# The second feed-forward's weights are split in token chunks 1 to 4, parked in DRAM, and fetched in chunk 5

## The chip, the core and the metric

The kernel runs on one core of a Trainium2 chip. The metric is the device time in microseconds (us) of one execution; each kernel is timed in several runs, and the median is quoted. A profile is one execution of its own, and its span runs from the first instruction to the last.

The engines are named as the profile names them: PE is TensorE (matmuls), DVE is VectorE, ACT is ScalarE, POOL is GpSimd, and SP is SyncE, which issues the DMAs here. Every engine works through its own instructions in the order in which they are written; an instruction that waits for a semaphore holds up all that stand behind it on that engine.

## What is computed

Three blocks follow one another, on 2304 tokens (4 batches of 576) of width 512 (8 heads of 64):

```python
q_s = softmax(q, axis=-1);  k_s = softmax(k, axis=2)         # a linear attention
x   = einsum(q_s, einsum(k_s, v))                            # [2304, 512]
xn  = x / rms(x) * rms_g                                     # first feed-forward, 1536 wide
x   = (silu(xn @ w_gate) * (xn @ w_val)) @ w_out
h   = x @ w_in                                               # second feed-forward, 2048 wide
P   = a[0] + a[1]*h + a[2]*h**2 + a[3]*h**3
Q   = 1.0 + abs(b[0])*abs(h) + abs(b[1])*h**2
out = (P / (Q + 1e-6)) @ w_out2
```

The feed-forward weights come as float64 arrays, q, k and v as float32.

## The kernel before

**Precision.** A product of two float32 matrices is made of three matmuls: each operand is split into a high and a low half that TensorE multiplies exactly (type fp32r), and high x high, high x low and low x high add up in PSUM (`mm3`, `proj`, `emit_y`, `o_pe`). So every operand exists as two tiles: x as X[c][0] and X[c][1], the product of gate and value as uh and ul, the rational function's result as gh and gl.

**Weights.** A weight tile is 128 x 512. The first feed-forward has 36 of them (W1: gate g, value v and output o of 12 steps f), the second 32 (W2: i for w_in and o for w_out, of 16 steps). A tile is loaded as float64 words (512 KB), put into a slot of 4 KB per partition (`tag=f"s{i % N1}"`, 36 slots) and converted there: two operations on the words (`conv_exp` on ACT, `conv_low` on ACT or DVE), the sign and the joining of the words on DVE (`conv_sign`, `conv_join`), the high half on ACT or DVE (`conv_hi`) and the low half on POOL (`conv_lo`). The split form takes over the slot. Since W1 fills all 36 slots, W2's tiles come into slots whose W1 tile was read for the last time, which is in the last chunk.

**Chunks and steps.** The tokens go in 6 chunks of 384. Chunk 0 is written out by hand as a list of events (ORDER), with the conversion of all of W1 in it. Chunks 1 to 5 run a loop over 12 steps f (`u_step`): the group g of 12 matmuls, silu on ACT, the group vv of 12 matmuls, the product u on DVE, its halves uh (ACT) and ul (DVE; POOL in chunk 5), and then the projection y of the step before, 12 matmuls (`emit_y`). Into three positions of every step the attention of the next chunk is woven (`schedule`): maxima, exponentials and sums on DVE and ACT, the small matmuls kv, xq and xx on PE. Chunks 2 and 3 compute the k and v part for a new batch in two halves of four heads; kv of the first half stands in step 4, of the second half in step 5. All v of the batch's second half goes into the one tile `vt0`, so its load (`load_v`) stands behind the first half's kv. A chunk's y goes to DRAM (`y_d`).

In chunk 5 there is no next attention. At the start of every step `load_to` issues the loads of W2 whose slots are free, and `tick` (`conv_tick`) puts one conversion further in three places of the step. What is left of the conversion runs in the second feed-forward (`conv_steps`, one operation of DVE a step).

**Second feed-forward.** A loop over 96 steps s (6 chunks of 16): h (12 matmuls, `h_pe`), the rational function on ACT and DVE (`rational`, six operations on each), gh on ACT and gl on POOL (`c_split`), and three steps later the output o (9 matmuls, `o_pe`).

Nothing but the written order decides what runs next: there is no scheduler. In what follows, tile i of W2 in a chunk's staging is called tile n.

Of the kernel before, what the change touches and what calls it, by code (L numbers as in the profile page):

```python
# [9 lines left out]
F32 = mybir.dt.float32  # L10
# [37 lines left out]
def kernel(  # L48
# [30 lines left out]
    # ln's argument is kept inside the table's range for every float32 denominator  # L79
# [20 lines left out]

    def ps(name):
        return pw.tile([P, 512], F32, tag="pw", name=name)

# [7 lines left out]
    # a 4 KB slot for each tile, which its split form takes over from its float64 form  # L111
# [8 lines left out]
    done = dict.fromkeys(("load", "a", "b", "c"), 0)  # L120
# [18 lines left out]

    def words(i):  # L140
        raw = raws[i]
        return (
            raw.bitcast(U32).rearrange("p (m t) -> p m t", t=2),
            raw.bitcast(F32).rearrange("p (m t) -> p m t", t=2),
        )

    # float64 words (low, high) to float32, rounded
    def conv_exp(i):
        w, r = words(i)
        # the exponent's bias goes from 1023 to 127; what float32 can't hold goes to zero  # L150
        nc.scalar.activation(r[:, :, 1], r[:, :, 1], AF.Copy, scale=2.0 ** -112)
# [42 lines left out]
    def conv_tick(end):  # L194
        """One tile further in each of three stages."""
        a, b, c = (done[k] for k in "abc")
        go_b = b < a
        if c < b:
            conv_hi(c)
            conv_lo(c)  # L200
            done["c"] += 1
        if go_b:
            conv_sign(b)
        if a < min(end, done["load"]):
            conv_exp(a)
            conv_low(a)
            done["a"] += 1
        if go_b:
            conv_join(b)
            done["b"] += 1  # L210

    def conv_steps():
        """What is left of the conversion, one operation of the vector engine at a time."""
        a, b, c = (done[k] for k in "abc")
        for i in range(c, len(order)):
            if i >= a:
                conv_exp(i)
                conv_low(i)
                yield
            if i >= b:  # L220
                conv_sign(i)
                conv_join(i)
                yield
            conv_hi(i)
            conv_lo(i)

# [5 lines left out]
    # five 6 KB slots: this chunk's two halves, the next one's q, x, and halves  # L232
# [18 lines left out]
    def runs(c):  # L251
        """Pieces of a chunk by batch: (batch, offset in the chunk, first row, rows)."""
        t0, end = c * T, (c + 1) * T
        while t0 < end:
            b, s = divmod(t0, S)
            n = min(end - t0, S - s)
            yield b, t0 - c * T, s, n
            t0 += n
# [4 lines left out]
    # four heads at a time, as two pairs: row s of head h of a pair is on partition  # L263
    # D * h + s // SC
# [18 lines left out]
    # token TT * p + t of the chunk is on partition p, in column t * P + p when turned  # L283
# [176 lines left out]
    # 1 / rms by token: Newton's steps from the exponent's half  # L460
# [33 lines left out]
    # the same for every partition at once, where the vector engine has the time  # L494
# [53 lines left out]
    def with_bank(evs, name):  # L548
        """Tensor-engine parts into one bank, then the rest."""
# [21 lines left out]
    def schedule(c):  # L571
        """By position (three in a step of the first feed-forward): what to emit there."""
# [90 lines left out]
    def u_step(c, f, at_pos, tick, lo_eng):  # L663
# [7 lines left out]
        tick()  # L671
# [4 lines left out]
        tick()  # L676
# [3 lines left out]
        tick()  # L680

# [49 lines left out]
    def ab_dve(s0, s1):  # L731
        """The last three of step s0 and the first three of step s1, in turn."""
# [55 lines left out]
    with tc.manual_schedule():  # L788
        # the first chunk's attention, with the first weights behind it
# [9 lines left out]
        # the tensor engine's clock rises only under load  # L799
# [5 lines left out]
        # The first chunk, in ORDER: events of the attention of chunk 0 (a..), of chunk 1 (b..),  # L805
        # of the weights (l: load up to a tile, c..: conversion), and of the feed-forward's steps
# [54 lines left out]
        # attention, of batch 0 for chunk 0 and of batch 1 for chunk 1  # L861
# [23 lines left out]
        # chunk 0: x before its scaling by token serves the first two steps  # L885
# [62 lines left out]
        # chunk 1's x  # L948
# [12 lines left out]
        # chunk 0's steps  # L961
# [37 lines left out]
        done.update(a=N1, b=N1, c=N1)  # L999

        for c in range(1, NCH):
# [5 lines left out]
            else:  # L1007
# [7 lines left out]
                # the second one's first steps run under the end of the first  # L1015
# [3 lines left out]
            for f in range(F1):  # L1019
                tick = lambda: None  # L1020
                if last:
                    # into slots of tiles that an earlier step was the last to read
                    load_to(N1 + min(max(0, 3 * f - 1), 2 * F2))
                    tick = (lambda: conv_tick(len(order))) if f < F1 - 1 else (lambda: None)
# [3 lines left out]
        rest = conv_steps()  # L1028
        n_h = 3
        for s in range(2, len(steps) + 3):  # L1030
# [11 lines left out]
            if s > 2:  # L1042
                next(rest, None)
# [35 lines left out]
```

## Time and profile before

| | us |
|---|---|
| median of 3 runs | 1022.33 (1022.26 to 1022.91) |
| the profiled execution, span | 1019.5 |
| PE busy | 962.4 (94%) |
| DVE busy | 713.7 (70%) |
| ACT busy | 561.6 (55%) |
| POOL busy | 284.5 (28%) |
| chunk 0 | 0 to 167.4 |
| chunks 1, 2, 3, 4 start | 167.4, 246.9, 335.7, 424.5 |
| chunk 5 starts | 504.0 |

The profiled execution's own time is not listed apart from its span; the median of the runs is 2.8 us longer than the span. Matmuls are pipelined and their ends are modelled, so a busy PE may still not be one at its peak: the distance from the start of one matmul to the start of the next tells more than the busy time. The granted clock is TensorE's, 1.00 for 2.4 GHz and 0.5 for 1.2 GHz. An idle time of an engine in the rows stands in brackets with what ended it.

### The profile page before, as it was taken

How to read it: one execution, taken by the hardware profiler on the slowest of the kernel's cores; microseconds unless marked ns; L12 is line 12 of the kernel's file. 1: busy time of each engine (PE TensorE's matmuls, PEld its weight loads, DVE VectorE, ACT ScalarE, POOL GpSimd, SP SyncE). 2: the span in 40 equal slices, each digit the busy share in tenths (PEclk: the TensorE clock that was granted, in tenths of full speed). 3: DMA queues.
4: the chain of work that ended last, by engine and by line, in shares of the span. 5: the costliest groups of instructions: out<-in, count | busy, mean ns of one | idle time of the engine just before them, and what ended most of it. 6: DMA issues, size and time to landing. Idle time of an engine off the chain costs nothing.

```text
span 1019.5 us, 14130 instructions
## 1 busy us (share of the span) xinstructions
PE 962.4 (94%) x5408; PEld 896.2 (88%) x5408; DVE 713.7 (70%) x1160; ACT 561.6 (55%) x1037; POOL 284.5 (28%) x240
## 2 busy tenths in 40 slices
PE   7877779999999999999998889899999999999998
PEld 7775778999999999999997877699999999999997
DVE  5799996436535643633569989987777777777776
ACT  2565553322312232232244557788888888878876
POOL 2565534000000000000047753432423324224222
PEclk7799989999999999999999889999999999999999
DMA  8993002003010410100085521001010010100000
GB/s 213 352 312 114 1 1 69 18 1 78 32 48 1 109 25 1 47 16 1 32 280 183 166 63 63 1 1 63 1 63 1 1 63 1 40 23 1 32 1 31
DMA packets 57491, 64.87 MB, mean 64 GB/s; under 512 B 21328, under 2 KB 47952, under 8 KB 57424
## 3 DMA queue, kind: packets, MB, share of 16 engines
q1 hardware_dynamic: 57424, 63.98, 20.6%
q8 instruction: 42, 0.69, 0.3%
q14 instruction: 25, 0.20, 0.1%
HBM read 54.53 MB, written 9.44 MB: 63 GB/s over the span
## 4 chain that ended last, share of the span: by engine, by line
PE 70%; DVE 20%; issue 6%; ACT 2%; DMA 1%; POOL 0%; DVEq 0%; SPq 0%; ACTq 0%
DVE raw L165 6%; PE o L768 6%; PE o L767 6%; PE o L766 6%; PE h L615 6%; PE h L613 6%; PE h L614 6%; DVE tmp L172 4%; PE g L613 3%; PE vv L613 3%; PE vv L615 3%; PE g L615 3%; PE g L614 3%; PE vv L614 3%; PE y L614 3%
## 5 line engine op out<-in xcount | busy, mean ns | idle before, releaser
L754 POOL TENSOR_TENSOR gl<-t,gh 128x384 fp32r<-128x384 f32 x94 | 105.7, 1124 | 245.5 <-ACT gh L752 207.1
L615 PE MATMUL h<-y,w 128*128 128x384 f32 x384 | 129.5, 337 | 0.0
L613 PE MATMUL h<-y,w 128*128 128x384 f32 x384 | 129.3, 337 | 0.0
L614 PE MATMUL h<-y,w 128*128 128x384 f32 x384 | 128.9, 336 | 0.0
L190 POOL TENSOR_TENSOR w<-tmp,w 128x512 fp32r<-128x512 f32 x68 | 104.8, 1546 | 82.7 <-ACT w L184 41.4
L727 DVE SCALAR_TENSOR_TENSOR A<-S,absb,A 128x384 f32<-128x384 f32 x96 | 62.7, 653 | 80.8 <-ACT A L717 80.8
L768 PE MATMUL o<-w,gl 128*128 128x512 f32 x288 | 114.8, 399 | 3.3 <-POOL gl L754 3.2
L651 ACT ACTIVATE uh<-u 128x384 fp32r<-128x384 f32 x72 | 37.8, 525 | 145.4 <-DVE u L660 126.3
L766 PE MATMUL o<-w,gh 128*128 128x512 f32 x288 | 112.5, 391 | 2.3 <-ACT gh L752 2.3
L767 PE MATMUL o<-w,gh 128*128 128x512 f32 x288 | 113.7, 395 | 0.0
L614 PE MATMUL y<-ul,w 128*128 128x384 f32 x288 | 100.7, 350 | 11.7 <-POOL ul L656 7.3
L613 PE MATMUL y<-uh,w 128*128 128x384 f32 x288 | 101.7, 353 | 9.9 <-ACT uh L651 9.8
L660 DVE TENSOR_TENSOR u<-u,vv 128x384 f32<-128x384 f32 x60 | 33.1, 551 | 108.1 <-PE vv L615 95.8
L656 POOL TENSOR_TENSOR ul<-u,uh 128x384 fp32r<-128x384 f32 x18 | 21.2, 1180 | 306.0 <-ACT uh L651 305.8
L613 PE MATMUL g<-x,w 128*128 128x384 f32 x280 | 98.9, 353 | 3.3 <-DVE w L182 3.1
L615 PE MATMUL g<-x,w 128*128 128x384 f32 x280 | 96.2, 344 | 3.4 <-POOL w L190 3.4
L615 PE MATMUL y<-uh,w 128*128 128x384 f32 x288 | 99.3, 345 | 0.0
L614 PE MATMUL g<-x,w 128*128 128x384 f32 x280 | 96.2, 343 | 0.0
L667 ACT ACTIVATE u<-g 128x384 f32<-128x384 f32 x60 | 29.3, 488 | 102.0 <-PE g L615 102.0
L613 PE MATMUL vv<-x,w 128*128 128x384 f32 x240 | 81.1, 338 | 0.0
L615 PE MATMUL vv<-x,w 128*128 128x384 f32 x240 | 80.3, 335 | 0.0
L614 PE MATMUL vv<-x,w 128*128 128x384 f32 x240 | 80.2, 334 | 0.0
(190 smaller groups left out, 2389.1 us busy)
## 6 DMA issues: line engine op xcount, KB each, us to landing
raw<-in_moe_w_out_dram SPq DMA_DIRECT2D x28, 512.0 KB, 6.0
raw<-in_moe_w_in_dram SPq DMA_DIRECT2D x16, 512.0 KB, 4.2
raw<-in_moe_w_gate_dram SPq DMA_DIRECT2D x12, 512.0 KB, 9.3
raw<-in_moe_w_val_dram SPq DMA_DIRECT2D x12, 512.0 KB, 10.5
k<-in_k_dram SPq DMA_DIRECT2D x8, 576.0 KB, 5.7
v<-in_v_dram SPq DMA_DIRECT2D x16, 288.0 KB, 6.7
y_d<-y SPq DMA_DIRECT2D x6, 768.0 KB, 3.5
yr<-y_d SPq DMA_DIRECT2D x6, 768.0 KB, 4.5
```

The costliest lines, as they stand in the source:

```text
L165: nc.vector.tensor_scalar(out=h[:, :, 1], in0=h[:, :, 3], scalar1=0x8000, scalar2=None, op0=ALU.bitwise_and)
L172: nc.vector.scalar_tensor_tensor(out=tmps[i], in0=w[:, :, 1], scalar=3, in1=w[:, :, 0], op0=ALU.logical_shift_left, op1=ALU.bitwise_or,)
L190: nc.gpsimd.tensor_tensor(out=t[:, 1, :], in0=tmps.pop(i).bitcast(F32), in1=t[:, 0, :], op=ALU.subtract)
L613: nc.tensor.matmul(o, lhsT=lh, rhs=rh, start=start, stop=False)
L614: nc.tensor.matmul(o, lhsT=lh, rhs=rl, start=False, stop=False)
L615: nc.tensor.matmul(o, lhsT=ll, rhs=rh, start=False, stop=stop)
L651: nc.scalar.activation(uh, u, AF.Copy)
L727: nc.vector.scalar_tensor_tensor(out=out, in0=in0, scalar=scalar, in1=in1, op0=op0, op1=op1)
L754: eng.tensor_tensor(out=r["gl"], in0=r["t"], in1=r["gh"], op=ALU.subtract)
L766: nc.tensor.matmul(o, lhsT=r["gh"][:, ts], rhs=w[:, 0], start=first, stop=False)
L767: nc.tensor.matmul(o, lhsT=r["gh"][:, ts], rhs=w[:, 1], start=False, stop=False)
L768: nc.tensor.matmul(o, lhsT=r["gl"][:, ts], rhs=w[:, 0], start=False, stop=last)
```

## The change

W2 is no longer converted in chunk 5 and behind it. Chunk 0 ends with four stores (`park`) of the split W1 tiles in slots 0 to 3 (gate and value of steps 0 and 1) to DRAM. In each of chunks 1 to 4, once steps 0 and 1 have read these slots, eight tiles of W2 pass through them, one a step: load into slot 0 or 1 (`stage_load`), both operations on the words on ACT (`stage_words`), sign and join on DVE (`stage_join`), high half on ACT and low half on DVE into slot 2 or 3, and a store to DRAM (`stage_split`, `park`). A tile takes three steps. In steps 8 to 11 the four W1 tiles are fetched back for the next chunk. In chunk 5, `fetch_to` reads the split tiles from DRAM into the slots where `load_to` put the float64 words; `conv_tick` and `conv_steps` are gone. The number of matmuls is the same, and so are ORDER and the second feed-forward.

```diff
+    split_d = {}
...
-    done = dict.fromkeys(("load", "a", "b", "c"), 0)
+    done = {"load": 0}
...
+    def park(i, t):
+        split_d[i] = dram.tile([P, 2, 512], F32, name=f"sd_{i}")
+        nc.sync.dma_start(out=split_d[i], in_=t.bitcast(F32))
+
+    def fetch(i):
+        dct, which, f = order[i]
+        t = wp.tile([P, 2, 512], F32R, tag=f"s{i % N1}", name=f"wf_{i}")
+        nc.sync.dma_start(out=t.bitcast(F32), in_=split_d[i])
+        dct[which, f] = t
+
+    def fetch_to(n):
+        while done["load"] < n:
+            fetch(done["load"])
+            done["load"] += 1
...
-    def conv_tick(end):
...
-    def conv_steps():
...
+    PARK = 2 * F2 // (NCH - 2)
+
+    def stage_load(c, n):
+        i = N1 + PARK * (c - 1) + n
+        dct, which, f = order[i]
+        src = w_rows(w_out2, f) if which == "o" else w_cols(w_in2, f)
+        raw = wp.tile([P, 512], U64, tag=f"s{n % 2}", name=f"raw_{i}")
+        dst = raw.rearrange("p (c m) -> p c m", m=P) if len(src.shape) == 3 else raw
+        nc.sync.dma_start(out=dst, in_=src)
+        raws[i] = raw
+
+    def stage_words(c, n):
+        i = N1 + PARK * (c - 1) + n
+        conv_exp(i)
+        w, r = words(i)
+        nc.scalar.activation(w[:, :, 0], w[:, :, 0], AF.Copy, scale=7.49 * 2.0 ** -32)
+
+    def stage_join(c, n):
+        i = N1 + PARK * (c - 1) + n
+        conv_sign(i)
+        conv_join(i)
+
+    def stage_split(c, n):
+        i = N1 + PARK * (c - 1) + n
+        raws.pop(i)
+        t = wp.tile([P, 2, 512], F32R, tag=f"s{2 + n % 2}", name=f"ws_{i}")
+        nc.scalar.activation(t[:, 0, :], tmps[i].bitcast(F32), AF.Copy)
+        nc.vector.tensor_tensor(
+            out=t[:, 1, :], in0=tmps.pop(i).bitcast(F32), in1=t[:, 0, :], op=ALU.subtract
+        )
+        park(i, t)
+
+    def stage(c, f, part):
+
+        if part == 0 and 0 <= f - 2 < PARK:
+            stage_split(c, f - 2)
+        if part == 1:
+            if 0 <= f - 1 < PARK:
+                stage_words(c, f - 1)
+            if f < PARK:
+                stage_load(c, f)
+        if part == 2:
+            if 0 <= f - 1 < PARK:
+                stage_join(c, f - 1)
+            if PARK <= f < PARK + 4:
+                fetch(f - PARK)
...
-        tick()
+        tick(0)
...
-        tick()
+        tick(1)
...
-        tick()
...
+        tick(2)
...
-        done.update(a=N1, b=N1, c=N1)
+        for i, (which, f) in enumerate((("g", 0), ("v", 0), ("g", 1), ("v", 1))):
+            park(i, W1[which, f])
...
-                tick = lambda: None
                 if last:
-                    # into slots of tiles that an earlier step was the last to read
-                    load_to(N1 + min(max(0, 3 * f - 1), 2 * F2))
-                    tick = (lambda: conv_tick(len(order))) if f < F1 - 1 else (lambda: None)
+
+                    fetch_to(N1 + min(max(0, 3 * f - 1), 2 * F2))
+                tick = lambda part: None if last else stage(c, f, part)
...
-        rest = conv_steps()
...
-            if s > 2:
-                next(rest, None)
```

Three places of the built programs, all in chunk 2. First SP, around the load of v for the second half (`v_86`; `y_d` is the store of chunk 1's y, `k_0` and `q` are loads for the attention of the next chunk). Before:

```order
L643 DMA y_d<-y_2169 128x1536
L280 DMA v_86<-in_v_dram 128x9x64 x2
L271 DMA k_0_2875<-in_k_dram 128x2x576
L290 DMA q_2877<-in_q_dram 64x8x192 x2
L280 DMA v_86<-in_v_dram 128x9x64 x2
```

Now (`ws` and `sd` are a split tile and its place in DRAM, `raw` the float64 words):

```order
L678 DMA y_d<-y_2283 128x1536
L223 DMA raw_2334<-in_moe_w_out_dram 128x512
L145 DMA sd_2380<-ws_2377 128x1024
L223 DMA raw_2405<-in_moe_w_in_dram 128x4x128
L145 DMA sd_2443<-ws_2440 128x1024
L223 DMA raw_2468<-in_moe_w_out_dram 128x512
L145 DMA sd_2503<-ws_2500 128x1024
L223 DMA raw_2529<-in_moe_w_in_dram 128x4x128
L315 DMA v_86<-in_v_dram 128x9x64 x2
L145 DMA sd_2612<-ws_2609 128x1024
```

Between the store of y and the two loads of v stand three parks and four loads; the last park before v waits for the low half of `ws_2500`.

Second ACT, from uh of step 3 to uh of step 4 (`k_0`, `k_1` and `q` get their exponentials there). Before:

```order
L651 ACTIVATE uh_3_2321<-u_3_2302 128x384
L341 ACT_TABLE_LOAD
L341 ACTIVATE k_0_2114<-k_0_2114 128x1152
L341 ACTIVATE k_1_2120<-k_1_2120 128x1152
L388 ACTIVATE q_2116<-q_2116 128x1536
L667 ACT_TABLE_LOAD
L667 ACTIVATE u_4_2353<-g_4_2340 128x384
L651 ACTIVATE uh_4_2369<-u_4_2353 128x384
```

Now:

```order
L686 ACTIVATE uh_3_2459<-u_3_2435 128x384
L376 ACT_TABLE_LOAD
L376 ACTIVATE k_0_2226<-k_0_2226 128x1152
L376 ACTIVATE k_1_2232<-k_1_2232 128x1152
L423 ACTIVATE q_2228<-q_2228 128x1536
L169 ACTIVATE raw_2405<-raw_2405 128x512
L230 ACTIVATE raw_2405<-raw_2405 128x512
L702 ACT_TABLE_LOAD
L702 ACTIVATE u_4_2498<-g_4_2485 128x384
L241 ACTIVATE ws_2500<-tmp_2483 128x512
L686 ACTIVATE uh_4_2519<-u_4_2498 128x384
```

The words of one tile come between the exponential of q and the table load for silu, and its high half between silu and uh.

Third DVE, from the subtraction on q to the product u of step 3 (`k` minus its maximum stands between). Before:

```order
L383 TENSOR_TENSOR q_2116<-q_2116,mq_2192 128x1536
L660 TENSOR_TENSOR u_2_2254<-u_2_2254,vv_2_2256 128x384
L656 TENSOR_TENSOR ul_2_2272<-u_2_2254,uh_2_2270 128x384
L336 TENSOR_TENSOR k_0_2114<-k_0_2114,ks_3_2274 128x1152
L336 TENSOR_TENSOR k_1_2120<-k_1_2120,ks_3_2304 128x1152
L660 TENSOR_TENSOR u_3_2302<-u_3_2302,vv_3_2307 128x384
```

Now:

```order
L418 TENSOR_TENSOR q_2228<-q_2228,mq_2306 128x1536
L183 TENSOR_SCALAR raw_2269<-raw_2269 128x512
L190 SCALAR_TENSOR_TENSOR tmp_2360<-raw_2269 128x512
L242 TENSOR_TENSOR ws_2377<-tmp_2360,ws_2377 128x512
L695 TENSOR_TENSOR u_2_2375<-u_2_2375,vv_2_2382 128x384
L691 TENSOR_TENSOR ul_2_2398<-u_2_2375,uh_2_2396 128x384
L371 TENSOR_TENSOR k_0_2226<-k_0_2226,ks_3_2400 128x1152
L183 TENSOR_SCALAR raw_2334<-raw_2334 128x512
L190 SCALAR_TENSOR_TENSOR tmp_2420<-raw_2334 128x512
L371 TENSOR_TENSOR k_1_2232<-k_1_2232,ks_3_2437 128x1152
L242 TENSOR_TENSOR ws_2440<-tmp_2420,ws_2440 128x512
L695 TENSOR_TENSOR u_3_2435<-u_3_2435,vv_3_2445 128x384
```

Sign, join and subtraction of two tiles now stand ahead of u of step 3, and the subtraction of each waits for ACT's high half.

## Rows read from the trace of the kernel before

**Rows 1.** Busy by stage: us, PE, PEld, DVE, ACT, POOL, PEclk, DMA share, GB/s

```profile
246.90:335.70 88.80, 88.62 (x606) 86.13 (x605) 44.05 (x73) 25.32 (x46) 0.00 (x0) 1.00 0.16 46
...
520.60:661.90 141.30, 122.89 (x596) 110.57 (x595) 135.73 (x174) 86.33 (x162) 81.98 (x59) 0.94 0.35 115
```

**Rows 2.** Waits of PE, 520.6 to 661.9 us: us in total, times, longest

```profile
PE y L614 <- POOL ul L656: 6.7, 8, 1.1
PE y L613 <- ACT uh L651: 6.0, 6, 2.6
PE o L768 <- POOL gl L754: 3.2, 5, 0.8
PE o L766 <- ACT gh L752: 2.3, 4, 1.0
```

**Rows 3.** Timeline of PE: start, us, engine, line, operation, tiles, shape

```profile
167.40 0.33 PE L613 MATMUL g<-x,w 128*128 128x384 f32 x1
...
169.48 0.33 PE L613 MATMUL vv<-x,w 128*128 128x384 f32 x1
...
520.62 0.34 PE L613 MATMUL y<-uh,w 128*128 128x384 f32 x1
...
661.94 0.33 PE L613 MATMUL h<-y,w 128*128 128x384 f32 x1
...
699.60 0.33 PE L613 MATMUL h<-y,w 128*128 128x384 f32 x1
...
703.79 0.33 PE L613 MATMUL h<-y,w 128*128 128x384 f32 x1
```

**Rows 4.** Timeline of PE around 554 us, in chunk 5

```profile
551.99 0.44 PE L614 MATMUL y<-ul,w 128*128 128x384 f32 x1 [0.99 <-POOL ul L656]
...
552.97 0.52 PE L615 MATMUL y<-uh,w 128*128 128x384 f32 x1
...
556.09 0.34 PE L613 MATMUL g<-x,w 128*128 128x384 f32 x1
```

**Rows 5.** Timeline of DVE, in chunk 2 and in chunk 5

```profile
271.28 0.55 DVE L660 TENSOR_TENSOR u<-u,vv 128x384 f32<-128x384 f32 x1 [0.50 <-PE vv L615]
...
575.49 1.49 DVE L172 SCALAR_TENSOR_TENSOR tmp<-raw 128x512 uint32<-128x512 uint32 x1
576.91 0.75 DVE L165 TENSOR_SCALAR raw<-raw 128x512 uint16<-128x512 uint16 x1
...
577.84 0.67 DVE L172 SCALAR_TENSOR_TENSOR tmp<-raw 128x512 uint32<-128x512 uint32 x1
578.43 0.54 DVE L660 TENSOR_TENSOR u<-u,vv 128x384 f32<-128x384 f32 x1
```

**Rows 6.** Groups by line: ACT's operation on words, count, busy us, mean ns

```profile
L151 ACT ACTIVATE raw<-raw 128x512 f32<-128x512 f32 x68 | 44.3, 669 | 5.2 <-DMA raw<-in_moe_w_in_dram 5.2
```

**Rows 7.** Timeline of ACT in chunk 2, after uh of step 3

```profile
272.41 1.28 ACT L341 ACT_TABLE_LOAD   x1
...
278.61 0.49 ACT L667 ACTIVATE u<-g 128x384 f32<-128x384 f32 x1
```

**Rows 8.** Timeline of SP: issues in chunk 2 and in chunk 5

```profile
281.59 2.29 SPq L280 DMA_DIRECT2D v<-in_v_dram  x2
...
511.07 0.32 SPq L643 DMA_DIRECT2D y_d<-y  x1
511.48 0.39 SPq L132 DMA_DIRECT2D raw<-in_moe_w_in_dram  x1
```

**Rows 9.** Landing, by tile: v at 280 to 292 us, raw at 511.0 to 511.9

```profile
DMA to landing us min/median/max: 3.4/3.4/3.4
...
DMA to landing us min/median/max: 6.8/6.8/6.8
```

**Rows 10.** Chain of work that ended last: kv of the second half, chunk 2

```profile
289.75 3.81 PE kv L349 x72
```

**Rows 11.** DMA issues of the page: count, KB each, median us to landing

```profile
raw<-in_moe_w_val_dram SPq DMA_DIRECT2D x12, 512.0 KB, 10.5
```

More of the change, by code (lines that the diff above doesn't have):

```diff
@@ L192, in conv_lo @@
         )
-    def conv_tick(end):
[L196 to L210, printed above, removed]
-    def conv_steps():
[L214 to L225, printed above, removed]
+    PARK = 2 * F2 // (NCH - 2)
```

## The prediction

> **What bounds the kernel now.** I read the busy time by stage first, to see where TensorE has holes. In chunk 2 it has none: 88.62 of 88.80 us [rows 1]. After 662 us it has none either: pair follows pair of its two products, h and o, each 4.19 us [rows 3]. Between 520.6 and 661.9 us, which is most of chunk 5 and the first ten steps of the second feed-forward, it is busy for 122.89 of 141.30 us, at a mean granted clock of 0.94, and there VectorE is the full one (135.73 us) [rows 1]. So the kernel is bound by TensorE everywhere except there and in chunk 0, which the change leaves alone.
>
> What ends TensorE's waits in that stretch stands in the table of waits [rows 2]: the projection y waits for ul from POOL and for uh from ACT, the output o for gl and gh. Those are the two halves of each hidden tile, and they are late because VectorE, ACT and POOL also convert W2 there. The listed waits (18.2 us) are not the loss, since matmul ends are modelled; starts of matmuls are safer. In dense stretches a group of 12 matmuls of 0.173 us (g, vv, y) starts 2.08 us after the one before (167.40 to 169.48), and a pair of h and o takes 4.19 us (699.60 to 703.79) [rows 3]. From the y that starts at 520.62 to the h that starts at 661.94 [rows 3], the program has 11 y, 9 g, 9 vv, 3 h alone and 10 pairs of h and o: 32 x 2.08 + 10 x 4.19 = 108.5 us. It took 141.3 us. **The hole is 32.8 us**, and it includes a lower clock: after the wait that ends at 551.99 a matmul's record is 0.52 us long instead of 0.33, and the ten from 552.97 to 556.09 start 0.31 us apart instead of 0.17 [rows 3, 4], which is the level of 1.2 GHz in place of 2.4.
>
> **What the change removes.** All conversion after 504 us: in chunk 5 and in the second feed-forward's start nothing is left on VectorE, ACT or POOL but the work of the tokens. What waits then? In chunk 5 the path from vv to ul (u on VectorE, uh on ACT, ul on POOL) has the two groups g and vv of the next step and the y before it, 6.2 us, as cover, and u alone is 0.54 us [rows 5]; so I expect the density of chunk 2. In the second feed-forward, the pairs of 4.19 us after 662 us [rows 3] show that a step's six vector operations and six of ACT fit under TensorE's own work. Its first outputs have less of a lead: gl comes from POOL after gh, and o now arrives 24 us earlier. Of the 5.5 us that o waits for now [rows 2] I keep 0.6; the ends are 0 and 5.5, and I sit near the low end because the conversion between those operations is what made them late. Gain: 32.8 - 0.6 = **32.2 us**.
>
> The loads in chunk 5 become fetches of the same 512 KB, into the same slots at the same positions, on SP. They cost no engine time, and the first of them can go where the first load goes now, right behind the store at 511.07 [rows 8], while the first h comes at the end of chunk 5, some 80 us later: nothing, covered by the chunk's own matmuls.
>
> **What it adds to chunks 1 to 4.** Eight tiles per chunk, one a step. On VectorE: sign, join and a subtraction. Undisturbed, a sign takes 0.75 us, a join 0.67 us, and the next operation starts 0.59 us after the join's start [rows 5]. The subtraction of 128x512 on VectorE is not in the trace; the join has its shape and two inputs too, so I take its price (the upper end is the 1.49 us of a join beside POOL [rows 5], but POOL is busy for 0.00 us in chunk 2 [rows 1]). Some 1.8 us a tile, 14 us a chunk, beside 44 of 88.8 us [rows 1]. On ACT: three operations of the shape that takes 0.67 us [rows 6], 2 us a tile, 16 us a chunk beside 25.32 us [rows 1]. Averaged, both stay under TensorE. So the price, if any, is a local one, in the attention that chunks 2 and 3 compute for 3 and 4. In chunks 1 and 4 the steps are lighter and I cost the addition at nothing: the 6.2 us between vv and its y hides two operations on each engine.
>
> I followed chunk 2 by hand at the place where VectorE and ACT are fullest, steps 2 to 5. In before, u of step 3 starts at 271.28 after 0.50 us of waiting [rows 5]. Two tiles stand ahead of it now: 2 x 1.75 us, and 0.7 us in which VectorE waits for ACT's high half of the first tile (the second one's is covered by a subtraction of k), less the 0.50: it moves by 3.7 us. The table load for exp, which follows uh on ACT, moves from 272.41 to 276.1. From there to the end of silu ACT has work without a hole, 272.41 to 279.10 [rows 7], 6.7 us; into it the change puts two words operations, 1.3 us, and behind it the high half (0.67) and VectorE's subtraction (0.67). So the low half of the tile is there at 276.1 + 9.3 = 285.4. The y of steps 2 and 3 still get their halves in time, with about 0.2 us to spare; the first kv gets its exp of k about 1 us before it needs it.
>
> **SP is where it shows.** In SP's queue the park of that tile waits for the subtraction, and behind it stand the load of tile 4 of the chunk and then the two loads of v for the second half. In before these v went out from 281.59, as soon as the first kv had read the buffer, landed 3.4 us after issue, and kv of the second half starts at 289.75 [rows 8 to 10], with nearly 5 us in hand. Now they go out after 285.4, at about 286.3, behind 1 MB of fresh traffic. The nearest row for that: a load of 512 KB issued 0.4 us after the store of 768 KB at 511.07 took 6.8 us [rows 8, 9], so 1.25 MB were through 7.2 us after the first issue. Park, load and first v are 1.28 MB: 285.4 + 7.2 = 292.6. TensorE stands at kv from 289.75 on, and behind it in its queue everything else. Bounds per chunk: 0 us (v alone, 286.3 + 3.4 = 289.7) and 4.4 us (1.5 us later, if the hand work above is off by that much). I take 2.5 us, by the row with the same bytes. Twice, for chunks 2 and 3: 5.0 us. What is queued behind is late by as much and finds more lead, so nothing is paid twice.
>
> [...]
>
> Clock: the wait of 0.99 us at 551.99, with another just before it, was followed by a stretch of half clock, in which the ten matmuls to 556.09 took 3.1 us in place of 1.7: 1.4 us more [rows 4]. A single stall of 2.5 us may or may not do this. I take one of the two: 1.4 us, ends 0 and 3.
>
> **The sum.** Against the profiled execution's span of 1019.5 us: 1019.5 - 32.2 + 5.0 + 1.4 = 993.7. The median of the runs is 2.8 us above that span (1022.33), as start and end lie around it: **996.5 us**, 2.5% faster.
>
> **Rivals.**
> *The v loads stay hidden.* If the store and the load ahead overlap better than the row of 511 us, or ACT's string is shorter, v lands near 290 and only 0 to 1 us is lost in each chunk. For it: landings of 3.4 us when alone [rows 9]. Against: the order in SP's queue is certain. Time: 1022.3 - 32.2 + 0 to 2 = 990 to 992. [...]
> *More waits in chunks 1 to 4.* The y of steps 2 to 5 have hardly any lead left by my reckoning. If every handoff is 0.3 us longer, u, uh and ul of four or five steps in chunks 2 and 3 come 1 us late each, with clock drops, and v another 1.5 us: 8 us more, about 1005. For it: VectorE and ACT there wait for each other three times a step. Against: TensorE's stall gives the lead back.
> *Slower.* The staging is a ring of two slots: load, words, join, high, subtraction, park, and only then the next load but one. That is the landing time plus some 4 us, within two steps (12.5 us); it decides from landings of 8.6 us on, since words block ACT and sign blocks VectorE. Each further us costs half a us in 32 steps, 16 us; above 10.6 us the gain is gone, and at 11.5 us it gives 990 + 46 = 1036. Loads in the burst of chunk 0 took 10.5 us in the median [rows 11], but with several in flight; here two are.
> *The hole stays.* The change would not do what it says if the waits of y and o came from the product's own path (uh on ACT, ul on POOL) and not from conversion ahead of it. Then the 18.2 us of listed waits [rows 2] remain, 14.6 us are gained and the stalls of chunks 2 and 3 come on top: 1022.3 - 14.6 + 6.4 = 1014. Against: joins of up to 1.49 us stand ahead of u in VectorE's order there [rows 5], and they go.
>
> **How the numbers follow.** Forecast (994 to 1001) 0.47; v hidden (990 to 993) 0.24; more waits (1001 to 1012) 0.20; hole stays (1010 to 1020) 0.05; slower 0.04. The range takes the first two and half of the third: 989.5 to 1005. A run of this kernel can tell a difference from about 0.2%, 2 us. Faster by more than that 0.94, within 0.02, slower 0.04.
>
> **What would show it.** Right: no wait for uh or ul after 520 us, the clock at 1.0 there, the stretch from y to h near 109 us; in chunks 2 and 3 one wait of 2 to 3 us at kv of the second half, ended by the DMA of v; chunks 1 and 4 without a wait. Wrong: waits at y in every step of chunks 1 to 4, or ACT waiting for the raw tiles (the ring is late), or no wait at kv (then it is 990).

## The result and the profile after

The changed kernel takes 998.53 us (median of 4 runs, 993.33 to 1000.46), the kernel before 1022.62 us beside it. The ratio is 0.9758, with a 95% interval of 0.9731 to 0.9785. The prediction was 996.5 us, from 989.5 to 1005. The profiled execution took 999.16 us, with a span of 997.4 us. One of the four runs of e9 below took 4810.47 us, at a granted clock of 0.186, and is left out of e9's figures.

The busy time by stage answers to [rows 1]. The first two lines are chunks 2 and 3, from the first g of a chunk to the first g of the next; the third is the stretch that was the hole, from the same y to the same h as in [rows 3]. Columns as in [rows 1].

```profile
247.26:343.73 96.47, 93.51 (x606) 90.68 (x605) 59.97 (x97) 38.55 (x70) 0.00 (x0) 0.95 0.48 151
343.73:435.10 91.37, 88.83 (x613) 87.25 (x613) 59.99 (x97) 38.54 (x69) 0.00 (x0) 1.00 0.51 153
...
531.27:639.82 108.55, 108.55 (x595) 104.33 (x595) 46.50 (x85) 53.54 (x104) 29.01 (x27) 1.00 0.43 149
```

The stretch that took 141.3 us takes 108.55 us, TensorE is busy in all of it at a clock of 1.00, and VectorE has gone from 135.73 us to 46.50. That is the gain. The price stands in the other two lines: from its first g to that of the next, chunk 2 took 88.77 us before and takes 96.47, chunk 3 took 88.71 and takes 91.37 (before, chunks 2, 3 and 4 start at 246.96, 335.73 and 424.44). Chunks 1 and 4 start 79.56 and 79.53 us before the next one, against 79.56 and 79.54: they cost nothing.

TensorE's waits from chunk 1 to chunk 4 (us in total, times, longest):

```profile
PE kv L384 <- DMA v<-in_v_dram: 3.4, 2, 1.9
PE vv L648 <- DVE u L695: 1.7, 2, 0.8
PE kt L351 <- DVE m L345: 0.4, 2, 0.2
```

Behind 505 us the same list is empty, where the kernel before waits for uh, ul, gh and gl [rows 2]. The timeline of TensorE shows the two kinds of wait, once in chunk 2 and, in its fourth row, once in chunk 3, and behind the first wait of kv the half clock (matmul records of 0.52 us, the level of 1.2 GHz, as in [rows 4]):

```profile
270.23 0.45 PE L648 MATMUL vv<-x,w 128*128 128x384 f32 x1 [0.85 <-DVE u L695]
...
293.11 5.96 PE L384 MATMUL kv<-v,k 64*64 64x65 f32 x72 [1.93 <-DMA v<-in_v_dram]
...
299.48 0.52 PE L649 MATMUL g<-x,w 128*128 128x384 f32 x1
...
389.14 0.24 PE L384 MATMUL kv<-v,k 64*64 64x65 f32 x1 [1.51 <-DMA v<-in_v_dram]
```

How long the half clock lasts is seen in the stretch in which it was granted (columns as in [rows 1]):

```profile
294.27:304.51 10.24, 10.24 (x73) 10.02 (x69) 3.63 (x9) 2.58 (x6) 0.00 (x0) 0.50 0.28 105
```

SP's queue at that place, answering to [rows 8] (start, us, instruction):

```profile
285.96 0.33 SPq L145 DMA_DIRECT2D sd<-ws  x1
286.33 0.43 SPq L223 DMA_DIRECT2D raw<-in_moe_w_in_dram  x1
286.85 1.93 SPq L315 DMA_DIRECT2D v<-in_v_dram  x2
```

VectorE there, answering to [rows 5]: the low halves of two tiles, the first with the product u of step 2 behind it.

```profile
269.01 0.69 DVE L242 TENSOR_TENSOR ws<-tmp,ws 128x512 fp32r<-128x512 f32 x1 [0.70 <-ACT ws L241]
269.62 0.55 DVE L695 TENSOR_TENSOR u<-u,vv 128x384 f32<-128x384 f32 x1
...
285.24 0.69 DVE L242 TENSOR_TENSOR ws<-tmp,ws 128x512 fp32r<-128x512 f32 x1 [0.86 <-ACT ws L241]
```

The low half ends at 285.93, its park goes out at 285.96, a load behind it, and v only at 286.85; v lands at 292.97 and kv starts at 293.11, 2.27 us after the last matmul of y. The other wait lies 23 us earlier in the same chunk: u of step 2 ends at 270.17 and vv of step 3 starts at 270.23. It takes over a PSUM buffer that u is the last to read.

The account against the kernel before, from starts of matmuls in the two profiled executions (a gap is counted less the 0.17 us that lie between matmuls anyway): the stretch up to chunk 5 is 10.35 us longer (167.70 to 514.63 against 167.40 to 503.98). Of it kv's waits are 2.1 and 1.7, vv's 0.95 twice, and the rest, 4.65, the clock (e0 below has nearly the same waits without the half clock, and its chunk 2 is 4.7 us shorter). Chunk 5 and what follows is 32.8 us shorter (482.8 against 515.5).

### The profile page after: what moved, and what is told of

It reads as the page before. It is cut to its first block, busy times and chain, and to the rows that moved or that the text cites. A ratio compares the mean times of both kernels' runs of the same rounds, so it can differ in the third digit from the quotient of the medians.

```text
span 997.4 us, 14266 instructions
## 1 busy us (share of the span) xinstructions
PE 955.3 (96%) x5408; PEld 896.3 (90%) x5408; DVE 683.4 (69%) x1160; ACT 579.5 (58%) x1069; POOL 230.8 (23%) x208
## 4 chain that ended last, share of the span: by engine, by line
PE 84%; DVE 12%; issue 2%; DMA 2%; ACT 0%; DVEq 0%
PE h L650 7%; PE o L803 7%; PE h L648 7%; PE o L802 7%; PE h L649 7%; PE o L801 7%; PE g L648 4%; PE g L649 4%; PE g L650 4%; PE vv L648 4%; PE vv L649 4%; PE vv L650 4%; PE y L649 4%; PE y L650 4%; PE y L648 4%; DVE raw L183 3%
## 5 line engine op out<-in xcount | busy, mean ns | idle before, releaser
L650 PE MATMUL h<-y,wf 128*128 128x384 f32 x384 | 129.5, 337 | 0.0
L648 PE MATMUL h<-y,wf 128*128 128x384 f32 x384 | 129.3, 337 | 0.0
L649 PE MATMUL h<-y,wf 128*128 128x384 f32 x384 | 128.9, 336 | 0.0
L803 PE MATMUL o<-wf,gl 128*128 128x512 f32 x288 | 114.1, 396 | 0.0
L802 PE MATMUL o<-wf,gh 128*128 128x512 f32 x288 | 113.7, 395 | 0.0
L801 PE MATMUL o<-wf,gh 128*128 128x512 f32 x288 | 112.0, 389 | 0.0
L648 PE MATMUL y<-uh,w 128*128 128x384 f32 x288 | 98.7, 343 | 2.7 <-ACT uh L686 2.7
L649 PE MATMUL y<-ul,w 128*128 128x384 f32 x288 | 96.7, 336 | 3.9 <-DVE ul L691 3.3
L691 POOL TENSOR_TENSOR ul<-u,uh 128x384 fp32r<-128x384 f32 x18 | 19.2, 1065 | 338.8 <-ACT uh L686 338.7
L650 PE MATMUL y<-uh,w 128*128 128x384 f32 x288 | 96.3, 335 | 0.0
L648 PE MATMUL g<-x,w 128*128 128x384 f32 x248 | 87.8, 354 | 3.4 <-DVE w L200 3.1
L650 PE MATMUL g<-x,w 128*128 128x384 f32 x248 | 85.9, 347 | 3.1 <-POOL w L208 3.1
L649 PE MATMUL g<-x,w 128*128 128x384 f32 x248 | 85.5, 345 | 0.9 <-DVE x L962 0.9
L183 DVE TENSOR_SCALAR raw<-raw 128x512 uint16<-128x512 uint16 x68 | 60.2, 913 | 24.2 <-ACT raw L230 23.5
L648 PEld LDWEIGHTS h<-y,wf 128*128 128x128 f32 x384 | 72.2, 188 | 4.1
L649 PEld LDWEIGHTS h<-y,wf 128*128 128x128 f32 x384 | 72.1, 188 | 4.0
L648 PE MATMUL vv<-x,w 128*128 128x384 f32 x208 | 70.7, 340 | 1.7 <-DVE u L695 1.7
## 6 DMA issues: line engine op xcount, KB each, us to landing
raw<-in_moe_w_val_dram SPq DMA_DIRECT2D x12, 512.0 KB, 10.5
```

Of the source, the lines that this page charges most:

```text
L183: nc.vector.tensor_scalar(out=h[:, :, 1], in0=h[:, :, 3], scalar1=0x8000, scalar2=None, op0=ALU.bitwise_and)
L648: nc.tensor.matmul(o, lhsT=lh, rhs=rh, start=start, stop=False)
L649: nc.tensor.matmul(o, lhsT=lh, rhs=rl, start=False, stop=False)
L650: nc.tensor.matmul(o, lhsT=ll, rhs=rh, start=False, stop=stop)
L801: nc.tensor.matmul(o, lhsT=r["gh"][:, ts], rhs=w[:, 0], start=first, stop=False)
L802: nc.tensor.matmul(o, lhsT=r["gh"][:, ts], rhs=w[:, 1], start=False, stop=False)
```

## Experiments

Times are medians; the kernel before, run beside them, took 1022.58 us with e0 to e3, 1022.49 with e4 to e7 and 1021.95 with e8 and e9.

**e0: the changed kernel once more.** No edit; a second profile, to see which parts of the price return.

> The changed kernel once more, as the measure for the three that follow. The theory (the two loads of v behind the park and the load in SP's queue make the second kv wait in chunks 2 and 3, and in chunk 2 the clock falls after that) expects 993 to 1000 us again, with one wait of about 2 us at kv in each of chunks 2 and 3 and one of about 1 us at vv of step 3; whether the half clock follows in chunk 2, in chunk 3, in both or in neither differs from run to run, 4.4 us each, which is why the runs of this kernel spread over 7 us. The rival (the kernel waits there because VectorE and ACT are full, and SP's order is of no weight) expects the same time and says nothing on the spread.

999.65 us (993.23 to 1000.8). The profiled execution took 993.23 us. Its chunks 2 and 3 by stage:

```profile
245.83:337.59 91.76, 88.87 (x606) 86.15 (x605) 59.95 (x97) 38.58 (x70) 0.00 (x0) 1.00 0.51 158
337.59:429.15 91.56, 88.82 (x613) 87.24 (x613) 59.97 (x97) 38.56 (x69) 0.00 (x0) 1.00 0.51 152
```

Its timeline of TensorE at the kv that waits in chunk 2, and one g after it:

```profile
291.59 3.85 PE L384 MATMUL kv<-v,k 64*64 64x65 f32 x72 [1.85 <-DMA v<-in_v_dram]
...
295.64 0.34 PE L649 MATMUL g<-x,w 128*128 128x384 f32 x1
```

Nearly the same waits (kv starts 2.19 us after the last matmul of y, against 2.27), but no half clock: the 72 matmuls of kv take 3.85 us instead of 5.96, the g's record is 0.34 us long instead of 0.52, and chunk 2 is 4.7 us shorter. So the waits return in both profiles (5.8 us in all), and the fall of the clock does not. Of the 6 us between these two executions of one kernel, 4.7 are the fall of the clock behind kv's wait and 1.4 lie in chunk 0 (166.27 us against 167.70); that the other six runs differ for the same reasons is likely, but they left no trace.

**e1: park and load behind v.** The park and the next load are issued in part 2 of the step, behind the loads of v in SP's queue.

```diff
-        park(i, t)
+        parked.append((i, t))
...
+        if part == 2:
+            if parked:
+                park(*parked.pop())
             if f < PARK:
                 stage_load(c, f)
-        if part == 2:
```

> Park and load of every step are issued behind the loads of v, no operation of VectorE or ACT moves. Theory: v goes out near 281.6 us as in the kernel before, lands 3.4 us later, kv of the second half doesn't wait (2.1 and 1.6 us back), the clock stays at 1.0 there (4.4 us back); 991 us, and the runs lie closer together. Rival (VectorE and ACT are what kv waits for): v is early and kv still waits 1 to 2 us, for exp of k or for its bank; 996 to 998. The wait of 1 us at vv of step 3 stays by both.

989.86 us (989.65 to 990.03), ratio 0.9682 (0.9666 to 0.9697). SP's queue in chunk 2:

```profile
281.99 2.29 SPq L318 DMA_DIRECT2D v<-in_v_dram  x2
284.96 0.33 SPq L146 DMA_DIRECT2D sd<-ws  x1
```

Chunks 2 and 3 by stage:

```profile
246.26:336.14 89.88, 88.85 (x606) 86.17 (x606) 59.87 (x97) 38.67 (x70) 0.00 (x0) 1.00 0.51 162
336.14:425.94 89.80, 88.77 (x614) 87.23 (x614) 59.89 (x97) 38.63 (x69) 0.00 (x0) 1.00 0.51 156
```

v goes out at 281.99 as in [rows 8] and lands at 285.26; kv doesn't wait, and the clock stays at 1.00. Both were the price of the order in SP's queue, 8.7 us of the median (9.8 against e0, which ran beside e1). The four runs now lie within 0.4 us. What is left over 88.8 us is 1.0 us a chunk, the wait of vv, which is untouched.

**e2: the load alone behind v.** As e1, but the park stays ahead of v.

> Only the load of the next tile goes behind v; the park, with its wait for VectorE's low half, stays ahead. Theory: v goes out 0.4 us earlier than now, near 286.4, with 0.5 MB ahead instead of 1 MB, and lands some 1.8 us earlier, near 291.2: kv waits about 0.4 us in chunk 2 and not at all in chunk 3, no half clock; 992 us. If only the time of issue counts and not the traffic ahead, v lands near 292.6 and kv still waits 1.7 us; 997. If only the traffic counts, it is as in the kernel before: no wait.

990.21 us (989.84 to 990.75), ratio 0.9686 (0.967 to 0.9701). The park goes out at 284.77 and v right behind it:

```profile
285.19 1.51 SPq L315 DMA_DIRECT2D v<-in_v_dram  x2
```

v lands at 289.40, 4.2 us after its issue, and kv starts at 289.89 without a wait; I had expected 291.2, a short wait and 992 us. With the landings of e1 and of the changed kernel this prices what is ahead of v: nothing ahead 3.3 us, the store of 512 KB ahead 4.2 us, store and load ahead 6.1 us. The store cost v 0.9 us and the load 1.9; in chunk 3 the three landings are 3.9, 4.2 and 5.7 us, so both prices are lower there (0.4 and 1.5). The wait for the low half (3.2 us later than in e1) and the store's traffic still fit into the lead: what the changed kernel loses at kv needs the load ahead of v as well, and e2 wins it back with the park left where it was.

**e3: the low half behind u as well.** As e1, and the split of a tile moves from part 0 to part 1, so that u of the step stands ahead of it on VectorE.

```diff
-        if part == 0 and 0 <= f - 2 < PARK:
-            stage_split(c, f - 2)
         if part == 1:
+            if 0 <= f - 2 < PARK:
+                stage_split(c, f - 2)
```

> As the one with v first, and the high and low half of the tile are made behind the step's product u and not ahead of it. Theory: u no longer waits for ACT's high half and for a subtraction, so vv of step 3, whose PSUM bank u of step 2 has to free, doesn't wait (1.0 us back in each of chunks 2 and 3): 989 us, no wait over 0.4 us on TensorE in chunks 1 to 4. Rival (VectorE is full in steps 2 to 4 whatever the order): the wait of about 1 us stays or goes to y of steps 2 to 4; 991.

991.11 us (990.91 to 995.44), ratio 0.9704, against 989 expected: not better than e1. The rival's 991 came, but not by its wait. The waits of vv are gone and chunk 2 is back at 88.76 us, but a new one is there at the end of the attention. SP's queue ahead of chunk 3:

```profile
329.42 0.32 SPq L146 DMA_DIRECT2D sd<-ws  x1
329.80 4.01 SPq L151 DMA_DIRECT2D wf<-sd  x3
333.86 0.43 SPq L309 DMA_DIRECT2D k<-in_k_dram  x1
```

VectorE there, the eighth tile's low half and the maximum of the k that was loaded:

```profile
328.71 0.68 DVE L243 TENSOR_TENSOR ws<-tmp,ws 128x512 fp32r<-128x512 f32 x1
...
340.97 2.22 DVE L348 TENSOR_REDUCE m<-k 128x128 f32<-128x1152 f32 x1 [3.98 <-DMA k<-in_k_dram]
```

TensorE in chunk 3, where it needs that maximum:

```profile
350.36 0.33 PE L354 MATMUL kt<-ident,m 128*128 128x128 f32 x1 [2.14 <-DVE m L348]
```

The eighth tile's low half now stands behind the norm on VectorE and comes at 328.71; its park holds SP's queue until 329.42 (321.44 in e1), and three fetches and the load of k for the next attention are queued behind it. k lands at 340.95 instead of 330.74, its maximum is late, and TensorE waits for it at 350.36, with 3.4 us of half clock after it. It is the mechanism of v once more, with k in its place.

**e4: as e3, but the eighth tile as in e1.**

```diff
+        if part == 0 and f - 2 == PARK - 1:
             stage_split(c, f - 2)
         if part == 1:
+            if 0 <= f - 2 < PARK - 1:
+                stage_split(c, f - 2)
```

> The kernel with v first and u first lost in chunk 3 what it gained: its eighth tile's halves stood behind the long norm on VectorE, so its park, three fetches and the load of k behind them on SP came 8 us later, and kt of chunk 3 waited 2.5 us. Here the eighth tile is split where it was, the other seven behind u. Theory: the wait at vv of step 3 is gone in chunks 2 and 3 (1.0 us each against v first alone, 989.9 us), k is back near 331 us, and no new wait comes: 988.0 us. Rival (VectorE is so full there that the microsecond turns up at y or at kt): 989 to 991 us.

988.05 us (987.2 to 988.64), ratio 0.9664 (0.9648 to 0.9679). Chunks 2 and 3:

```profile
245.85:334.62 88.77, 88.59 (x605) 86.09 (x605) 59.87 (x97) 38.51 (x70) 0.00 (x0) 1.00 0.52 163
334.62:423.34 88.72, 88.54 (x613) 87.19 (x613) 59.88 (x97) 38.53 (x69) 0.00 (x0) 1.00 0.53 157
```

That is the length of before [rows 1], with the whole conversion of W2 in it. This version beats both kernels, the changed one by 10.5 us. The two waits of vv were worth 1.8 us of the median (989.86 - 988.05), and 2.2 us by the lengths of the two chunks (89.88 and 89.80 in e1).

**e5, e6, e7: what made the hole.** On top of e1 (which has no wait nearby), operations on scratch tiles are put back into steps 0 to 10 of chunk 5, three times a step: in e5 sign, low word and join on VectorE, in e6 a subtraction of 128x512 on GpSimd, in e7 both, independent of one another.

Of e6 and e7:

```diff
+        nc.gpsimd.tensor_tensor(out=p, in0=p.bitcast(F32), in1=p, op=ALU.subtract)
```

Of e5 and e7:

```diff
+        nc.vector.tensor_scalar(
+            out=h[:, :, 1], in0=h[:, :, 3], scalar1=0x8000, scalar2=None, op0=ALU.bitwise_and
+        )
+        nc.vector.tensor_scalar(
+            out=w[:, :, 0], in0=w[:, :, 0], scalar1=2.0 ** -29, scalar2=7.0,
+            op0=ALU.mult, op1=ALU.min,
+        )
+        t = wp.tile([P, 512], U32, tag="tmp", name="xtmp", bufs=2)
+        nc.vector.scalar_tensor_tensor(
+            out=t, in0=w[:, :, 1], scalar=3, in1=w[:, :, 0],
+            op0=ALU.logical_shift_left, op1=ALU.bitwise_or,
+        )
```

> On the kernel with v first (989.9 us); its output isn't used by what is added. In steps 0 to 10 of chunk 5 VectorE does again what a conversion cost it, three times a step: sign, low word, join of 128x512, on a scratch tile; POOL and ACT get nothing. This asks what made the hole of 24 us in chunk 5. Theory (VectorE and POOL slow each other down: a join of 0.67 us takes 1.5 beside POOL): alone the nine operations take some 4.6 us of a step of 6.2, u is late by 1 us at most, under cover: 990 to 992 us. Rival (VectorE's own operations were too many): most of the hole is back, 1005 us or more.

> As the one before, with POOL's part instead of VectorE's: three subtractions of 128x512 a step, on a scratch tile. Theory: POOL has 3 x 1.4 and ul, 5.4 us, in a step of 6.2; ul is late by up to 1.5 us, under cover: 990 to 993 us. Rival (POOL alone makes ul late, since most waits in chunk 5 were listed as ended by ul): 1000 us or more.

> Both parts, VectorE's nine and POOL's three operations a step in chunk 5, with no dependence between the two. Theory (contention): the two together cost far more than the sum of each alone: single operations of VectorE last 1.2 to 1.8 us beside POOL's, its step goes past 6.2 us and half or more of the hole of 24 us comes back, with half clock: 1002 to 1014 us. Rival (the sum counts): the sum of the two above, under 995 us; then the hole came from the loads, from ACT or from the chain between the three engines.

| | us | against e1 | from the y to the h of [rows 3] |
|---|---|---|---|
| e1 | 989.86 | | 108.56 |
| e5, VectorE | 997.4 (996.44 to 998.37) | +7.5 | 114.96 |
| e6, GpSimd | 990.22 (989.72 to 990.72) | +0.4 | 108.55 |
| e7, both | 1018.86 (1018.22 to 1019.18) | +29.0 | 138.04 |

The same window of each, columns as in [rows 1]; first e5:

```profile
522.00:638.00 116.00, 112.08 (x601) 105.22 (x601) 106.18 (x169) 53.58 (x106) 30.09 (x28) 1.00 0.42 138
```

e6:

```profile
522.00:638.00 116.00, 116.00 (x635) 111.33 (x635) 52.54 (x95) 58.63 (x114) 58.35 (x57) 1.00 0.44 144
```

e7:

```profile
522.00:638.00 116.00, 97.36 (x486) 90.40 (x485) 109.05 (x138) 34.52 (x69) 56.72 (x48) 0.94 0.42 142
```

VectorE alone costs a quarter of what both cost, GpSimd alone next to nothing, and both together 29 us, nearly four times the sum of the parts. e6 came out as expected; e5 (990 to 992 expected) and e7 (1002 to 1014) cost more than that. Why both together cost so much is seen in e7's timeline of VectorE around 557 us:

```profile
554.77 0.43 DVE L282 TENSOR_SCALAR xraw<-xraw 128x512 uint32<-128x512 uint32 x1
555.23 0.69 DVE L287 SCALAR_TENSOR_TENSOR xtmp<-xraw 128x512 uint32<-128x512 uint32 x1
...
557.07 1.23 DVE L282 TENSOR_SCALAR xraw<-xraw 128x512 uint32<-128x512 uint32 x1
558.34 1.41 DVE L287 SCALAR_TENSOR_TENSOR xtmp<-xraw 128x512 uint32<-128x512 uint32 x1
```

GpSimd at the same time:

```profile
557.02 1.00 POOL L720 TENSOR_TENSOR ul<-u,uh 128x384 fp32r<-128x384 f32 x1 [4.09 <-ACT uh L715]
557.98 2.67 POOL L276 TENSOR_TENSOR xp<-xp 128x512 fp32r<-128x512 f32 x2
```

In the 4.09 us in which GpSimd is idle, up to its product's half at 557.02, VectorE's operations take 0.43 and 0.69 us; beside it the same two take 1.23 and 1.41, and GpSimd's subtraction, 1.04 us on average in e6, averages 1.29. Not every operation of VectorE is stretched: u, which reads one of its inputs from PSUM, takes 0.55 us in e6 in the four steps in which GpSimd works beside all of it, as in the nine others. With both engines stretched, u is late, and y waits for uh and ul as in [rows 2] (e7's waits of TensorE between 505 and 662 us):

```profile
PE y L677 <- ACT uh L715: 12.8, 8, 2.3
PE y L678 <- POOL ul L720: 5.7, 9, 0.6
```

The miss of e5 fits the same rows: a set of three takes VectorE 1.86 us undisturbed (553.98 to 555.84 in e7), so three sets and u nearly fill a step of 6.2 us, where I had 4.6 us for the sets, and in e5 too GpSimd's ul stretches some of them (10 of 33 low words took 1.2 us, 5 of 33 joins 1.4). That this makes the whole 7.5 us is not shown.

How much of the hole this explains is seen at the h right behind the last y of the first feed-forward, in the kernel before, the changed kernel and e7:

```profile
611.42 0.33 PE L613 MATMUL h<-y,w 128*128 128x384 f32 x1
...
597.84 0.33 PE L648 MATMUL h<-y,wf 128*128 128x384 f32 x1
...
617.10 0.52 PE L677 MATMUL h<-y,wf 128*128 128x384 f32 x1
```

From the same y on (520.62, 531.27 and 521.76) that is 90.8, 66.6 and 95.3 us. So 24.2 us of the 32.8 lie ahead of this h, and there VectorE's and GpSimd's extra operations beside each other are enough: they cost 28.8, with 33 sets where the kernel before ran some 28. The other 8.5 us lie at the first outputs of the second feed-forward, where e7 puts nothing back and loses 0.7; so 138.04 us in all, close to the 141.3 of before, is no proof that the whole hole is explained. The operations of e7 are not those of before one by one either (three equal sets a step, and ACT's conversion was not put back), so what the single operations of before cost stays open, and which of them made the waits for gl and gh.

**e8: the low half on GpSimd again in chunks 1 to 4**, all else as in the changed kernel. **e9: the same on top of e1.**

```diff
-        nc.vector.tensor_tensor(
+        nc.gpsimd.tensor_tensor(
             out=t[:, 1, :], in0=tmps.pop(i).bitcast(F32), in1=t[:, 0, :], op=ALU.subtract
```

> The changed kernel with one thing undone: in token chunks 1 to 4 the low half of each parked tile is made on GpSimd again instead of VectorE (order of issue as in the changed kernel, the fifth chunk unchanged). Theory: VectorE has no low half ahead of u in steps 2 and 3 of chunks 2 and 3, so vv waits less for u (1.12 us twice in the changed kernel); the park waits for GpSimd's slower low half, so v lands some 0.4 us later and kv's wait of about 2 us in chunks 2 and 3 stays or grows to 2.5; the time is some 997 us (991 to 999, by whether the clock falls). Rival: VectorE's work beside GpSimd is slowed as in e7, u comes later and vv waits as long or longer: 1000 us or more.

> e1 (parks and loads behind v) with the low half of chunks 1 to 4 on GpSimd instead of VectorE. Theory: no wait of kv for v and none of vv for u, so chunks 2 and 3 fall from 89.9 to some 88.9 us each and the time to some 988 us, as in e4. Rival: GpSimd beside VectorE slows the signs, u and the gates, and the time is 990 us or more.

e8: 1002.41 us (1000.03 to 1002.52), ratio 0.981 (0.9794 to 0.9827), against 997 expected. e9: 988.43 us (988.11 to 988.44), ratio 0.9672 (0.9656 to 0.9688), as expected. e8's chunks 2 and 3 by stage:

```profile
246.05:340.11 94.06, 91.67 (x606) 89.09 (x606) 56.23 (x89) 38.56 (x70) 11.53 (x10) 0.96 0.49 154
340.11:435.94 95.83, 92.99 (x613) 91.55 (x613) 56.23 (x89) 38.55 (x70) 11.54 (x10) 0.95 0.48 146
```

e8's timeline of TensorE at kv in both chunks:

```profile
291.02 3.27 PE L384 MATMUL kv<-v,k 64*64 64x65 f32 x50 [2.20 <-DMA v<-in_v_dram]
...
385.55 0.66 PE L384 MATMUL kv<-v,k 64*64 64x65 f32 x4 [2.65 <-DMA v<-in_v_dram]
```

The low half on GpSimd in e8:

```profile
267.91 1.30 POOL L242 TENSOR_TENSOR ws<-tmp,ws 128x512 fp32r<-128x512 f32 x1 [35.88 <-ACT ws L241]
```

What VectorE does beside it:

```profile
268.28 1.34 DVE L691 TENSOR_TENSOR ul<-u,uh 128x384 fp32r<-128x384 f32 x1 [0.65 <-ACT uh L686]
```

My theory's mechanism held in its first half: no vv waits in e8 or e9, which is why the two chunks of e9 are back at 88.78 and 88.72 us, the result of e4 by another way. The rival's mechanism, vv as late as before, did not show, though e8's time lies on its side of the line. The sum failed on what it left: without its wait for u TensorE reaches kv 1.1 us earlier in the chunk, v lands only 0.9 us earlier (I had it 0.4 us later), so kv's waits grew (2.20 and 2.65 us, from 1.93 and 1.51), and the clock fell behind both of them (0.96 and 0.95), not behind none or one. In chunk 3 the changed kernel waits less (1.51 us) than e0 at the same place (starts of matmuls 1.85 and 2.05 us apart), so part of that growth is the difference between two runs. A wait that is taken away ahead of a later one is here partly handed on to it.

## Why the prediction was right, and where its terms were off

**The hole.** Right: 141.3 - 108.5 worked out from starts of matmuls, 108.55 measured. Of the 0.6 us that I kept for the first outputs hardly 0.1 is there. e5 to e7 bear out the reason, conversion ahead of u, for chunk 5, with one correction: the words "VectorE is the full one" are half of it. With e5's operations on VectorE alone the hole is 6.4 us (114.96 - 108.55), and GpSimd's beside them make it 29.5. For the outputs of the second feed-forward the reason is borne out only by what the change itself removed. The rival that the hole stays fell.

**kv behind SP's queue.** The mechanism and the place were right, and e1 shows it as the cause. By hand the low half was to be there at 285.4 and v at 292.6; measured are 285.93 and 292.97, with the chunk itself 0.3 us later than before. From the park's issue to the landing 7.0 us passed, close to the row of 7.2. A tile's three operations take VectorE 2.0 us (272.50 to 273.90 and 275.16 to 275.76), not 1.75. By my own figures the wait would have been 2.85 us (292.6 - 289.75); I took 2.5 and gave no reason for the difference. It came out at 2.1 and 1.7 us, since TensorE itself reached kv some 1 us later: it had waited for u. And of what stood ahead of v, the load decided (e2), not the park's wait alone.

**vv behind u: missed.** The step that failed is the one that says the y of steps 2 and 3 still get their halves in time. They do, no y waits there. But I followed u only to its reader, y, and not to what u sets free: the PSUM buffer that the next step's vv needs. u of step 2 has one tile's sign, join and low half ahead of it, and vv loses 0.95 us for it, in chunk 2 and in chunk 3. e4 and e9 remove it in two ways and gain 1.8 and 1.4 us.

**The clock: mis-sized.** I took one fall of 1.4 us, with ends of 0 and 3, from a row in which ten matmuls ran at the low level. In the profiled execution there was one fall, but TensorE stayed at 1.2 GHz for 10.24 us, which cost 4.65. The other profiled execution of the same kernel had none, and e8 two. I read the length from too short a row: the trace of before also has a stretch of 6.83 us at 0.50, from 590.11 on.

The four terms together: 0.6 + 5.0 + 1.4 = 7.0 us expected, 0.1 + 3.8 + 1.9 + 4.65 = 10.4 in one profile and about 5.8 in the other. The forecast of 996.5 lies between the two kinds of run, 2 us under the median. That it lies so close is in part luck, for the errors go both ways: against the first profile the clock is 3.25 us too low, vv 1.9 and chunk 0 0.3, while kv is 1.2 us too high, the first outputs 0.5, and start and end 1.0 (that execution is 1.8 us longer than its span, not 2.8).

**The rest.** Chunks 1 and 4 at nothing: right. The ring of two slots: its loads landed in 4.2 and 4.6 us in the median and in 5.8 at most, far from the 8.6 from which it would have decided (the group of w_out below mixes 12 loads of chunk 0 with the ring's 16). Fetches at nothing: right, no h or o waits for them. "More waits" was there in one place and with 1.9 us, not 8. "v hidden" did not happen, but its 990 to 992 is what e1 and e2 give, where v is let past.

```profile
raw<-in_moe_w_out_dram SPq DMA_DIRECT2D x28, 512.0 KB, 5.3
raw<-in_moe_w_in_dram SPq DMA_DIRECT2D x16, 512.0 KB, 4.6
```

(Groups of the page of after: count, KB each, median us from issue to landing.)

## What to carry to other kernels

Work that crowds one stage can move into stages where the bounding engine is full, where the other engines have room there on average; here the gain could be read off the starts of matmuls before anything was run. What was left to look for were local prices, and the largest stood in a queue: a store that waits for an engine holds every load behind it in the same queue, and traffic issued ahead makes the load land later, so issue what the bounding engine waits for first (here worth 8.7 us for a few moved lines). When an operation is delayed, follow both its result and the buffers that it sets free.

## What the runs showed of the hardware

- VectorE and GpSimd slowed each other down in some operations: 0.43 to 1.23 us and 0.69 to 1.41 us for two operations of VectorE on 128x512 tiles in e7, and ul took 1.34 us beside GpSimd's low half in e8, where it took 0.56 on average in the changed kernel; u, with one input in PSUM, kept its 0.55 us beside GpSimd in e6. Costs measured on each alone (7.5 and 0.4 us) don't add up to that of both (29.0).
- A wait of about 2 us in a dense stretch was followed by 10.24 us at 1.2 GHz in one execution and by none in another of the same kernel; it cost more than the wait itself, 4.65 against 2.1 us. By starts of matmuls around the single waits of chunks 2 and 3, the clock fell behind 2.27 us (10.24 us at 1.2 GHz), 2.48 (3.41, e3), 2.54 and 2.99 (6.83 and 10.24, e8), and not behind 1.85, 2.05 and 2.19 (the changed kernel and e0). Seven cases are no rule.
- Ahead of a load of 288 KB in the same queue, a store of 512 KB cost it 0.9 us and a further load of 512 KB 1.9 us in chunk 2 (3.3, 4.2 and 6.1 us to landing in e1, e2 and the changed kernel); in chunk 3 it was 0.4 and 1.5 us.
